# A state-space scan and a squared-ReLU FFN on one core: the first weight issue waits for the first x, the clamped later rows lie in PSUM, and the third unit's loads are let in later

## Chip, cores, metric

The kernel runs on one core of a Trainium2 chip. The metric is device time in microseconds of one execution; lower is better. Engines are called PE (TensorE), DVE (VectorE), ACT (ScalarE), POOL (GpSimd) and SP (SyncE, which here only issues DMAs).

## What is computed

Inputs are x (4 batches, 8 heads, 768 positions, 32 channels), a decay a, and B and C with 16 state elements each; then w_in (256 by 2048) and w_out (2048 by 256). Everything is float32.

```python
for c in range(nc):                              # chunks of 32 positions
    cum = np.cumsum(log(clip(a, 1e-6, 1)), -1)   # per chunk
    L = np.exp(cum_i - cum_j) * causal
    y = (C B^T * L) x + (C state) * exp(cum)
    state = exp(sum) * state + sum_j (B_j x_j) * exp(cum_end - cum_j)
h = np.maximum(y @ w_in, 0.0)                    # y as (3072, 256)
out = h * h @ w_out
```

## The kernel before

The sequence is cut into 12 **units**: 4 batches by 3 blocks of 256 positions, in the order of `UNITS` (first block of all four batches, then the second, then the third). Units 0 to 3 carry no incoming state. The decay enters as running products, not as exponents: `clamp` (L617) limits a to 1e-6..1, `scan` (L546) multiplies along 128 positions into `cp`, PE turns `cp` into columns (`prep_p`, L520 to L530), and the result `P_sb` and its reciprocal `Pinv` scale C and x. The rows of a come in two sets: 64 rows for the first block (`a_cl[0]`, `ac0`, `sk0`) and 128 rows for the later two blocks (`a_cl[1]`, `ac1`, `sk1`).

For one unit k the steps are: load C, B and x (`ldC`, `ldB`, `ldx`, tiles C_nat, B_nat, x_nat); multiply C by the decay and cast B into the tile `jt` (`pc`, L168, and `pb`, L176/L180); transpose `jt` on PE (`tr`, L206) and copy it to `bct` (`tc`, L219/L221); scores on PE (`mt`, L236); mask them, directly from PSUM on DVE (`mk`, L245) or from a copy `sc` (`sc`, L250, then `ms`, L254); scale x (`px`, L188, tile `xs`); the unit's own state (`u`, L261); the spread state `Sd` (`sf`, L389); intra matmuls in two halves (`ina`, `inb`) and the carried state (`ca`), all L261; copy the result to `T` (`t`, L219). Then the FFN of the unit's 256 positions in eight tiles: `a0` is tile 0 of unit 0's first matmul (L452, weights w_in_b) with its ReLU on ACT (L473), `qa0` the square on DVE (L479), `A0` the second matmul (L452, weights w_out_b). Unit 1 uses b and B, and so on. `id` are PE fillers on constants (L553).

Every engine runs its instructions in the order of the string `ORDER`; each token is one step, and a letter behind a colon names the engine. The order is therefore written by hand, and an engine that waits holds everything behind it. DMAs of C, B and x go out on SP's queue (a few on ACT's), those of the weights on POOL's, which converts to bf16 on the way: `wi0` to `wi3` are w_in_b0 to w_in_b3 (L149), `wo0` to `wo3` are w_out_b0 to w_out_b3 (L153).

Two devices delay a DMA on purpose. A **gate** (`gC2`, L144) clears one column of a unit's tile on DVE ahead of the load into that tile, so that the load cannot go out before DVE has come to that place. **After** (`afC2`, L669) copies one column of a loaded tile on POOL, so that what stands behind it on POOL waits for the load.

PSUM has eight banks in one tile `pp`; bank 4 holds the first block's decays (`P0`, columns 0 to 63) and sums (columns 64 to 71) until the token `fr`.

Of the kernel before, what the change touches and what calls it, by code (L numbers as in the profile page):

```python
# [10 lines left out]
FP32 = mybir.dt.float32  # L11
# [19 lines left out]
def kernel(  # L31
# [16 lines left out]
    ORDER = """  # L48
        fa1:a jz0:v ef jz1:p id3:512 ti fa0:s la0:s id4:512 pi eb ldB0:s ac0:v ldC0:a sk0 ku sp la1:a pbh0:p hd
        id1:256 pc0:v pbl0:v mb:a id2:512 trC0 ps iv:8:16 tcC0:1:a tcC0:0:v trB0 la2:s tcB0:2:v pk id1:512 iv1:0:8  # L50
        id1:512 ldx0:s mt0 wi0 la3:s px0:v ldC1:s su id2:512 ldB1:s wi1 ldx1:s u0:67 mk0 fq mk0 gC2:v mk0 ac1:v pc1:p sc0
        pb1:a jz2:a id2:512 tr1 id3:512 tc1:1:a tc1:0:v to ms0:p sf0 sk1 wo0 wi2 px1:p mt1 ina0 inb0 ca0 pp1:a mk1 mk1 t0:aa
        sc1 us0 mk1 fr p2@4 a0 ldC2:s a1 u1::6 ina1 ms1:v wo1 wi3 pc2 inb1 sf1 ca1 pd t1:va us1 a3@0 qa1 ldB2:s
        qa0 a2@1 wo2 b0@2 qa3 qb0 b1@3 qb1 b2@4 b3@5 A0 A1 B0 pb2:p B1 tr2 zb0 qb3 gB3:v ldx2:s ldB3:s ldC3:s ldx3:s b4 a4
        iv:32:64 zb1 tc2:1:v qa2 tc2:0:v b5 sb1 sb0 qb4 a5 qb2 qa4 mt2 sc2 B3 iv:16:32 px2 pc3 wo3 px3 mk2 mk2 sc2 A3
        A2 ms2:v ms2:v qa5 a6 b6 pb3:a B2 a7 qb5 qa6 b7 u2 ina2 inb2 sf2 ld4 A4 tr3 ca2 tc3:1:v t2:aa B4 us2 B5
        tc3:0:v u3:45 pc4 mt3 A5 us3 sc3 c5 qb7 qb6 mk3 za3 pb4 ldC5:s ldB5:s c3 qa7 c4 qc5 c0 qc3 px4 tr4 ldx5:s pb5
# [17 lines left out]
    const = ctx.enter_context(tc.tile_pool(name="const", bufs=1))  # L75
# [22 lines left out]
    spread = const.tile([128, 128], FP32, name="spread")  # L98

    a_nat = [const.tile([n, 128], FP32, name=f"a_nat{n}") for n in (64, 128)]  # L100
    a_cl = [const.tile([n, 128], FP32, name=f"a_cl{n}") for n in (64, 128)]
    cp = [const.tile([n, 128], FP32, name=f"cp{n}") for n in (64, 128)]
    pick_p = [const.tile([n, m], FP32, name=f"pick_p{n}") for n, m in ((64, 8), (128, 16))]
    P_sb = const.tile([128, 2, 96], FP32, name="P_sb")
# [5 lines left out]
    w_out_b = [wpool.tile([128, 4, 256], BF16, name=f"w_out_b{i}") for i in range(4)]  # L110

    pp = psum.tile([128, 8, 512], FP32, name="pp")

    def total(i, b, j):
        return 4 * i + b if j == 0 else 4 + 8 * i + 4 * j + b
# [757 lines left out]
```

## Time and profile before

| | |
|---|---|
| median of 3 runs | 114.65 us |
| lowest, highest run | 113.89, 118.19 us |
| span of the profiled execution, first to last instruction | 117.0 us |
| PE, DVE, ACT, POOL busy in it | 108.8, 85.9, 77.2, 49.6 us |
| mean granted PE clock | 0.985 |
| HBM read, written | 10.58, 3.15 MB |

No time of the profiled execution other than its span is on record, so the span stands for it; it lies 2.35 us above the median of the runs and within their reach.

A timeline row has the start, the duration, the engine, the line (L188 is line 188 of the listing), the operation, output <- inputs with shapes, the count of merged instructions, and in brackets the idle time of the engine just before it with what ended that. SPq and POOLq are the engines' DMA issues. In a row of a stretch (28.00:30.00) stand the length, then for PE, weight loads, DVE, ACT and POOL the busy time with the number of instructions, then the granted PE clock, the busy share of the DMA engines and GB/s. A row of a DMA issue ends in KB and the median microseconds from issue to landing. A row of the chain has start, length and what was worked on; the chain is followed back from the last instruction through what released each step.

### The profile page before, as it was taken

What the parts mean: (1) busy time and instruction counts of PE and PEld (TensorE: products, weight loads), DVE (VectorE), ACT (ScalarE), POOL (GpSimd) and SP (SyncE); (2) the same over time, 40 slices, a digit from 0 to 9 for tenths busy, and PEclk for the clock granted to TensorE, in tenths of its full rate; (3) what the DMA queues carried; (4) which work ended last, traced back from release to release, by engine and by line L of the source; (5) the groups of instructions that cost most, each with busy time, mean ns of one, the idle gap of its engine ahead of it and who ended that gap; (6) DMA issues with size and microseconds to landing.
All of it is one profiled execution on the core that took longest, in us unless ns stands there. A gap on an engine that the chain in (4) does not pass through costs nothing.

```text
span 117.0 us, 3689 instructions
## 1 busy us (share of the span) xinstructions
PE 108.8 (93%) x1453; PEld 92.9 (79%) x1453; DVE 85.9 (73%) x190; ACT 77.2 (66%) x159; POOL 49.6 (42%) x95
## 2 busy tenths in 40 slices
PE   7995998992999999999999999999999999999990
PEld 2542796882599898998998989989989889899980
DVE  2699965999469589799966799949849678544540
ACT  1582992972479478569566886786687777876740
POOL 7699434398088062396054294444333020000000
PEclk9999999999599999999999999999999999999999
DMA  2999999799997807697599737699790020020202
GB/s 44 200 208 147 201 205 223 139 217 161 94 169 101 236 6 107 72 215 85 75 171 98 137 104 93 71 191 97 124 198 34 0 98 0 0 95 0 88 2 90
DMA packets 67281, 13.44 MB, mean 115 GB/s; under 512 B 63104, under 2 KB 65984, under 8 KB 67264
## 3 DMA queue, kind: packets, MB, share of 16 engines
q1 hardware_dynamic: 64320, 10.88, 56.1%
q0 software_dynamic: 1664, 2.10, 11.0%
q10 hardware_dynamic: 1280, 0.23, 1.0%
q8 instruction: 11, 0.18, 0.6%
q14 instruction: 6, 0.05, 0.1%
HBM read 10.58 MB, written 3.15 MB: 117 GB/s over the span
## 4 chain that ended last, share of the span: by engine, by line
PE 77%; DVE 10%; DMA 9%; issue 1%; POOL 0%; SPq 0%; ACT 0%; DVEq 0%; ACTq 0%
PE pp L452 64%; DMA B_nat<-in_B_dram 9%; PE pp L261 5%; DVE h L479 5%; PE pp L553 4%; PE pp L230 2%; DVE mts L245 2%; PE pp L236 1%; DVE bct L221 1%; DVE mts L254 1%; DVE xs L188 1%; PE pp L206 1%; PE pp L530 0%; DVE Pinv L647 0%; POOL jt L176 0%
## 5 line engine op out<-in xcount | busy, mean ns | idle before, releaser
L473 ACT ACTIVATE hb<-pp 128x512 bf16<-128x512 f32 x96 | 54.7, 602 | 24.1 <-PE pp L452 22.2
L479 DVE TENSOR_TENSOR h<-hb 128x512 bf16<-128x512 bf16 x96 | 46.6, 502 | 13.3 <-ACT hb L473 12.8
L452 PE MATMUL pp<-w_out_b,h 128*128 128x256 bf16 (+1 forms) x400 | 54.8, 272 | 0.0
L452 PE MATMUL pp<-T,w_in_b 128*128 128x256 bf16 x384 | 53.4, 273 | 0.1
L452 PEld LDWEIGHTS <-w_in_b 128*128 128x128 bf16 x384 | 41.5, 114 | 1.9 <-issue 1.1
L452 PEld LDWEIGHTS <-h 128*128 128x128 bf16 x400 | 38.1, 99 | 5.0 <-issue 1.2
L245 DVE TENSOR_TENSOR mts<-pp,mask 128x512 bf16<-128x512 f32 x43 | 28.5, 678 | 2.7 <-PE pp L236 1.9
L188 POOL TENSOR_TENSOR xs<-x_nat,Pinv 128x256 bf16<-128x256 f32 (+1 forms) x19 | 13.6, 733 | 11.4 <-DVE mts L245 4.0
L377 POOL TENSOR_TENSOR Sd<-z,Pquad 128x256 bf16<-128x256 f32 x16 | 10.4, 657 | 18.0 <-DVE z L361 12.8
L168 POOL TENSOR_TENSOR jt<-C_nat,P_sb 128x128 bf16<-128x128 f32 x22 | 9.9, 469 | 6.9 <-DMA C_nat<-in_C_dram 6.8
L553 PE MATMUL pp<-const-bfloat16-1.0 128*128 128x512 bf16 (+1 forms) x19 | 6.9, 492 | 0.8 <-PEq L857 0.8
L176 POOL CAST jt<-B_nat 128x256 bf16<-128x256 f32 x9 | 4.2, 466 | 7.9 <-DMA B_nat<-in_B_dram 7.9
L361 DVE SCALAR_TENSOR_TENSOR z<-z,Ptot,us 128x64 f32<-128x64 f32 x8 | 2.5, 312 | 6.8 <-ACT us L345 5.0
L261 PE MATMUL pp<-bct,Sd 128*128 128x128 bf16 x40 | 4.3, 224 | 2.5 <-DVE Sd L389 2.5
L501 ACT COPY osb<-pp 128x512 f32<-128x512 f32 x11 | 6.4, 582 | 0.3 <-PE pp L452 0.2
L261 PEld LDWEIGHTS <-Sd 128*128 128x128 bf16 x40 | 3.0, 98 | 3.1 <-DVE Sd L389 2.9
L261 PE MATMUL pp<-mts,xs 64*32 64x128 bf16 (+1 forms) x288 | 5.5, 219 | 0.0
L261 PEld LDWEIGHTS <-xs 64*32 64x32 bf16 (+1 forms) x288 | 3.6, 93 | 0.4 <-issue 0.2
L553 PEld LDWEIGHTS <-const-bfloat16-1.0 128*128 128x128 bf16 x19 | 1.8, 116 | 2.5 <-issue 2.2
L250 ACT CAST sc<-pp 128x512 bf16<-128x512 f32 x5 | 2.9, 606 | 0.5 <-PE pp L236 0.5
L149 POOL DMA_DIRECT2D w_in_b<-in_moe_w_in_dram x4 | 3.0, 759 | 0.3 <-issue 0.3
L261 PEld LDWEIGHTS <-jt 64*32 64x32 bf16 (+1 forms) x128 | 1.5, 91 | 2.1 <-issue 1.2
(76 smaller groups left out, 61.0 us busy)
## 6 DMA issues: line engine op xcount, KB each, us to landing
out_dram<-osb SPq DMA_DIRECT2D x11, 256.0 KB, 2.9
x_nat<-in_x_dram SPq DMA_DIRECT2D x6, 256.0 KB, 4.3
w_in_b<-in_moe_w_in_dram POOLq DMA_DIRECT2D x4, 256.0 KB, 6.6
w_out_b<-in_moe_w_out_dram POOLq DMA_DIRECT2D x4, 256.0 KB, 6.6
B_nat<-in_B_dram SPq DMA_DIRECT2D x6, 128.0 KB, 3.5
C_nat<-in_C_dram SPq DMA_DIRECT2D x12, 64.0 KB, 3.0
B_nat<-in_B_dram SPq DMA_DIRECT2D x12, 64.0 KB, 3.4
x_nat<-in_x_dram SPq DMA_DIRECT2D x6, 128.0 KB, 3.0
```

The source lines that it names most:

```text
L149: nc.gpsimd.dma_start(out=w_in_b[i], in_=_dap(moe_w_in, f0 * 256, [[2048, 128], [128 * 2048, 2], [1, n]]))
L168: eng.tensor_tensor(out=_fap(jt[k % 3], 128 + 144 * g, [[384, 2], [32, 4], [1, 16]]), in0=_fap(loaded[k]["C"], 128 * g, [[16, 2], [32, 4], ...
L176: fn(out=_fap(jt[k % 3], 0, [[384, 2], [16, 2], [32, 4], [1, 16]]), in_=_fap(loaded[k]["B"], 0, [[16, 2], [128, 2], [32, 4], [1, 16]]))
L188: eng.tensor_tensor(out=_fap(xs, 256 * r, [[256, 2 // n], [32, 8], [1, 32]]), in0=_fap(loaded[k]["x"], 32 * r, [[32, 2 // n], [64, 8], [1, ...
L245: nc.vector.tensor_tensor(out=live[k]["mts"][:, q].rearrange("p r g i -> p (r g i)"), in0=pp[:, q, :], in1=mask1 if k >= LATE else mask, o ...
L261: nc.tensor.matmul(dst, w, v, start=bool(need), stop=False, skip_group_check=True, **({} if pos is None else {"tile_position": pos}))
L377: nc.gpsimd.tensor_tensor(out=_fap(S_d, 0, [[128, 2], [32, 4], [1, 32]]), in0=_fap(z, 0, [[32, 2], [0, 4], [1, 32]]), in1=_fap(Pquad, 4 * ...
L452: nc.tensor.matmul(dst, w(0, 128), v, skip_group_check=True, **flags)
L473: nc.scalar.activation(out=hb.rearrange("p i t -> p (i t)"), in_=pp[:, h, :], func=AF.Relu)
L479: nc.vector.tensor_tensor(out=h2, in0=hb, in1=hb, op=ALU.mult)
L501: nc.scalar.copy(out=osb, in_=pp[:, 6 if blk == 1 else 7, :])
L553: nc.tensor.matmul(pp[:, h, 0:int(cols)], ones_b[:, 0:128], ones_b[:, 0:int(cols)] if dep is None else dep, start=True, stop=True, skip_gr ...
```

## The change

Five edits, four of them in the string `ORDER`:

- `afx0` is put ahead of `wi0`: POOL copies a column of x_nat0 before it issues the first weights.
- `a_cl[1]`, the clamped 128 rows, is no longer an SBUF tile but columns 256 to 383 of PSUM bank 4.
- `px1` (xs of unit 1) is put ahead of `wi2`, and `u1` (unit 1's own state) ahead of `a1`.
- `wo2` follows `wi3` at once, ahead of `pc2`, where it stood behind it.
- `gC2`, `ldC2` move from early places (between unit 0's masks; ahead of `a1`) behind `sf1`, unit 1's spread state. In SP's queue B and x of unit 2 stand behind C_nat2.

```diff
-        id1:512 ldx0:s mt0 wi0 la3:s px0:v ldC1:s su id2:512 ldB1:s wi1 ldx1:s u0:67 mk0 fq mk0 gC2:v mk0 ac1:v pc1:p sc0
-        pb1:a jz2:a id2:512 tr1 id3:512 tc1:1:a tc1:0:v to ms0:p sf0 sk1 wo0 wi2 px1:p mt1 ina0 inb0 ca0 pp1:a mk1 mk1 t0:aa
-        sc1 us0 mk1 fr p2@4 a0 ldC2:s a1 u1::6 ina1 ms1:v wo1 wi3 pc2 inb1 sf1 ca1 pd t1:va us1 a3@0 qa1 ldB2:s
-        qa0 a2@1 wo2 b0@2 qa3 ...
+        id1:512 ldx0:s mt0 afx0 wi0 la3:s px0:v ldC1:s su id2:512 ldB1:s wi1 ldx1:s u0:67 mk0 fq mk0 mk0 ac1:v pc1:p sc0
+        pb1:a jz2:a id2:512 tr1 id3:512 tc1:1:a tc1:0:v to ms0:p sf0 sk1 wo0 px1:p wi2 mt1 ina0 inb0 ca0 pp1:a mk1 mk1 t0:aa
+        sc1 us0 mk1 fr p2@4 a0 u1::6 a1 ina1 ms1:v wo1 wi3 wo2 inb1 sf1 gC2:v ldC2:s pc2 ca1 pd t1:va us1 a3@0 qa1 ldB2:s
+        qa0 a2@1 b0@2 qa3 ...
...
-    a_cl = [const.tile([n, 128], FP32, name=f"a_cl{n}") for n in (64, 128)]
+    a_cl = [const.tile([64, 128], FP32, name="a_cl64")]
...
+    a_cl.append(pp[:, 4, 256:384])
```

What POOL runs, from the cast of unit 0's B to the cast of unit 2's B, before (the number behind a tile's name tells its copies apart; w_in_b_113 to _116 are w_in_b0 to w_in_b3, w_out_b_117 to _119 are w_out_b0 to w_out_b2):

```order
L180 CAST jt_110<-B_nat_144 128x2x4x16
L149 DMA w_in_b_113<-in_moe_w_in_dram 128x2x512
L149 DMA w_in_b_114<-in_moe_w_in_dram 128x2x512
L168 TENSOR_TENSOR jt_111<-C_nat_207,P_sb 128x2x4x16 x2
L254 TENSOR_TENSOR mts_202<-sc_3_242,mask 128x512
L153 DMA w_out_b_117<-in_moe_w_out_dram 128x1024
L149 DMA w_in_b_115<-in_moe_w_in_dram 128x2x512
L188 TENSOR_TENSOR xs_267<-x_nat_215,Pinv 128x512
L153 DMA w_out_b_118<-in_moe_w_out_dram 128x1024
L149 DMA w_in_b_116<-in_moe_w_in_dram 128x2x512
L168 TENSOR_TENSOR jt_112<-C_nat_236,P_sb 128x2x4x16 x2
L153 DMA w_out_b_119<-in_moe_w_out_dram 128x1024
```

The same stretch of POOL in the changed kernel (w_in_b_112 to _115 are w_in_b0 to w_in_b3, w_out_b_116 to _118 are w_out_b0 to w_out_b2):

```order
L670 COPY gate_x_202<-x_nat_183 128x1
L150 DMA w_in_b_112<-in_moe_w_in_dram 128x2x512
L150 DMA w_in_b_113<-in_moe_w_in_dram 128x2x512
L169 TENSOR_TENSOR jt_110<-C_nat_208,P_sb 128x2x4x16 x2
L255 TENSOR_TENSOR mts_201<-sc_3_241,mask 128x512
L154 DMA w_out_b_116<-in_moe_w_out_dram 128x1024
L189 TENSOR_TENSOR xs_265<-x_nat_216,Pinv 128x512
L150 DMA w_in_b_114<-in_moe_w_in_dram 128x2x512
L154 DMA w_out_b_117<-in_moe_w_out_dram 128x1024
L150 DMA w_in_b_115<-in_moe_w_in_dram 128x2x512
L154 DMA w_out_b_118<-in_moe_w_out_dram 128x1024
L169 TENSOR_TENSOR jt_111<-C_nat_404,P_sb 128x2x4x16 x2
```

One copy has come in ahead of the first weights; xs1 has moved ahead of w_in_b2; and w_out_b2 ahead of unit 2's C product, so that four weight issues now stand in a row. (Lines count one higher in the changed kernel from L113 on.)

What DVE runs from unit 0's second mask to unit 1's copy of T, before (C_nat_236 is C_nat2, Sd_0_405 unit 1's spread state):

```order
L245 TENSOR_TENSOR mts_202<-pp,mask 128x512
L144 MEMSET C_nat_236 128x1
L245 TENSOR_TENSOR mts_202<-pp,mask 128x512
L617 TENSOR_SCALAR a_cl_101<-a_nat_99 128x128
L221 COPY bct_248<-pp 128x384
L389 TENSOR_TENSOR Sd_0_262<-pp,Pquad 128x256
L546 SCALAR_TENSOR_TENSOR cp_103<-a_cl_101,const-float32-0.0 128x128
L245 TENSOR_TENSOR mts_285<-pp,mask 128x512 x3
L254 TENSOR_TENSOR mts_285<-sc_2_326,mask 128x512
L389 TENSOR_TENSOR Sd_0_405<-pp,Pquad 128x256
L221 CAST T_411<-pp 128x4x64
```

And in the changed kernel (C_nat_404 is C_nat2):

```order
L246 TENSOR_TENSOR mts_201<-pp,mask 128x512 x2
L618 TENSOR_SCALAR pp<-a_nat_99 128x128
L222 COPY bct_247<-pp 128x384
L390 TENSOR_TENSOR Sd_0_261<-pp,Pquad 128x256
L547 SCALAR_TENSOR_TENSOR cp_102<-pp,const-float32-0.0 128x128
L246 TENSOR_TENSOR mts_284<-pp,mask 128x512 x3
L255 TENSOR_TENSOR mts_284<-sc_2_325,mask 128x512
L390 TENSOR_TENSOR Sd_0_402<-pp,Pquad 128x256
L145 MEMSET C_nat_404 128x1
L222 CAST T_413<-pp 128x4x64
```

The memset on C_nat2 has moved behind eight instructions, and the scan reads `pp` and the constant where it read two SBUF tiles. On PE the sixteen matmuls of u1 and the four of a1 change places; ACT's and SP's orders stay as they were.

More of the change, by code (lines that the diff above doesn't have):

```diff
@@ L50 @@
         id1:256 pc0:v pbl0:v mb:a id2:512 trC0 ps iv:8:16 tcC0:1:a tcC0:0:v trB0 la2:s tcB0:2:v pk id1:512 iv1:0:8
-        id1:512 ldx0:s mt0 wi0 la3:s px0:v ldC1:s su id2:512 ldB1:s wi1 ldx1:s u0:67 mk0 fq mk0 gC2:v mk0 ac1:v pc1:p sc0
-        pb1:a jz2:a id2:512 tr1 id3:512 tc1:1:a tc1:0:v to ms0:p sf0 sk1 wo0 wi2 px1:p mt1 ina0 inb0 ca0 pp1:a mk1 mk1 t0:aa
-        sc1 us0 mk1 fr p2@4 a0 ldC2:s a1 u1::6 ina1 ms1:v wo1 wi3 pc2 inb1 sf1 ca1 pd t1:va us1 a3@0 qa1 ldB2:s
-        qa0 a2@1 wo2 b0@2 qa3 qb0 b1@3 qb1 b2@4 b3@5 A0 A1 B0 pb2:p B1 tr2 zb0 qb3 gB3:v ldx2:s ldB3:s ldC3:s ldx3:s b4 a4
+        id1:512 ldx0:s mt0 afx0 wi0 la3:s px0:v ldC1:s su id2:512 ldB1:s wi1 ldx1:s u0:67 mk0 fq mk0 mk0 ac1:v pc1:p sc0
+        pb1:a jz2:a id2:512 tr1 id3:512 tc1:1:a tc1:0:v to ms0:p sf0 sk1 wo0 px1:p wi2 mt1 ina0 inb0 ca0 pp1:a mk1 mk1 t0:aa
+        sc1 us0 mk1 fr p2@4 a0 u1::6 a1 ina1 ms1:v wo1 wi3 wo2 inb1 sf1 gC2:v ldC2:s pc2 ca1 pd t1:va us1 a3@0 qa1 ldB2:s
+        qa0 a2@1 b0@2 qa3 qb0 b1@3 qb1 b2@4 b3@5 A0 A1 B0 pb2:p B1 tr2 zb0 qb3 gB3:v ldx2:s ldB3:s ldC3:s ldx3:s b4 a4
         iv:32:64 zb1 tc2:1:v qa2 tc2:0:v b5 sb1 sb0 qb4 a5 qb2 qa4 mt2 sc2 B3 iv:16:32 px2 pc3 wo3 px3 mk2 mk2 sc2 A3
```

## The prediction

> **What bounds the kernel now.** I read the page's busy rows first, then the chain in order of time, then the stretches where TensorE (PE) is idle.
>
> ```profile
> span 117.0 us, 3689 instructions
> PE 108.8 (93%) x1453; PEld 92.9 (79%) x1453; DVE 85.9 (73%) x190; ACT 77.2 (66%) x159; POOL 49.6 (42%) x95
> PE   7995998992999999999999999999999999999990
> ```
>
> PE is idle for 117.0 - 108.8 = 8.2 us. The third row (busy tenths, slices of 2.9 us) shows where: before the first matmul, behind the last, and in three dips, the slices that begin at 8.8 (5), 17.5 (8) and 26.3 us (2). From the eleventh slice on PE is full. The change touches only the first 15 us, so the question is what it does to the dips. Pieces of the chain:
>
> ```profile
> 8.91 10.07 DMA B_nat<-in_B_dram
> ...
> 19.04 0.44 POOL jt L176
> ...
> 24.51 2.74 DVE h L479 x2
> ...
> 27.33 1.76 DVE h L479
> ...
> 29.48 0.39 PE pp L261 x2
> ```
>
> The reader is to see two things. From 8.91 to 18.98 the chain is the load of the third unit's B (B_nat2): it lands, POOL casts it into jt2 (L176), PE transposes jt2 (L206, "tr2"), and from there the chain is mostly work of VectorE (DVE) up to 29.48, where PE takes over for good. So **what moves the landing of B_nat2 moves the end**, and what PE gains ahead of 19 us is waited away again at tr2.
>
> ```profile
> 19.04 0.43 POOL L176 CAST jt<-B_nat 128x256 bf16<-128x256 f32 x1 [3.32 <-DMA B_nat<-in_B_dram]
> 19.52 0.51 PE L206 MATMUL pp<-eye_b,jt 128*128 128x128 bf16 x6 [0.57 <-POOL jt L176]
> 28.00:30.00 2.00, 0.52 (x4) 0.46 (x5) 2.00 (x5) 0.56 (x3) 0.81 (x2) 0.81 2.03 190
> 30.00:32.00 2.00, 2.00 (x40) 1.14 (x38) 0.62 (x2) 0.55 (x3) 0.00 (x0) 0.50 0.53 51
> ```
>
> PE waits only 0.57 us at tr2 now. Its largest wait is the hole before 29.48 (PE busy 0.52 of 2.00 us), after which the granted clock (the column behind POOL's) falls to 0.50.
>
> **The change, part by part.**
>
> *The gate on the first weights.* POOL now copies one column of x_nat0 before it issues w_in_b0.
>
> ```profile
> 2.81 0.43 SPq L135 DMA_DIRECT2D x_nat<-in_x_dram  x1
> x_nat<-in_x_dram SPq DMA_DIRECT2D x1, 256.0 KB, 3.1
> 5.34 1.63 POOL L149 DMA_DIRECT2D w_in_b<-in_moe_w_in_dram  x2 [0.26 <-issue]
> 36.28 0.38 POOL L669 COPY gate_C<-C_nat 128x1 f32<-128x1 f32 x1
> 6.99 0.80 POOL L168 TENSOR_TENSOR jt<-C_nat,P_sb 128x128 bf16<-128x128 f32 x2
> 7.75 1.15 POOL L254 TENSOR_TENSOR mts<-sc,mask 128x512 bf16<-128x512 bf16 x1
> 8.17 0.50 PE L206 MATMUL pp<-eye_b,jt 128*128 128x128 bf16 x6
> ```
>
> x_nat0 lands at 2.81 + 3.1 = 5.9; the copy takes 0.38 by the like one at L669; so the first issue goes from 5.34 to 6.3, **0.95 us later**. Queued behind it on POOL are the second issue, unit 1's C product (L168: ends 8.75 instead of 7.8), the mask of the copied scores (L254) and w_out_b0. PE waits for the C product: unit 1's transposes go from 8.17 to about 8.8. The mask ends near 9.85 instead of 8.9; the matmuls that use it stand behind those transposes and unit 1's scores on PE (over half a microsecond of work and a copy in between), which cover it; uncovered it would cost the same 0.95 us in a place ahead of tr2. The first weights landed 6.1 us after issue, at 11.4 (row further down); now at 12.4, or sooner by up to 0.9 if x_nat1 leaves the DMA engines earlier.
>
> *The clamped rows in PSUM.* The scan (L546) loses one operand in SBUF.
>
> ```profile
> 3.06 0.43 DVE L546 TENSOR_TENSOR_SCAN cp<-a_cl,const-float32-0.0 64x128 f32<-64x128 f32 x1
> 9.72 1.81 DVE L546 TENSOR_TENSOR_SCAN cp<-a_cl,const-float32-0.0 128x128 f32<-128x128 f32 x1
> 10.17 1.07 POOL L188 TENSOR_TENSOR xs<-x_nat,Pinv 128x512 bf16<-128x512 f32 x1
> 11.67 0.42 PE L520 MATMUL pp<-eye_f,cp 128*64 128x16 f32 x8 [1.12 <-DVE cp L546]
> 12.45 1.03 PE L452 MATMUL pp<-T,w_in_b 128*128 128x256 bf16 x8
> ```
>
> The same number of elements per row took 0.43 us while POOL computed nothing and 1.81 us across POOL's 1.07 us product. I take 0.45 for the scan from PSUM, near the first row, on the reading that POOL's reads held up the second one (bounds 0.43 and 1.81). So the scan starts 0.65 later (behind unit 1's transposes), at about 10.4, and ends at 10.85 instead of 11.5. PE's second set of decays (L520) follows it, and 0.8 us behind that the first FFN matmul, which could start at 11.8 instead of 12.45; but w_in_b0 lands between 11.5 and 12.4. **Gain ahead of the first FFN matmul: 0 to 0.6 us, I take 0.2**, and it ends at tr2's wait.
>
> *xs1, the state matmuls u1 and w_in_b2's issue.* These change places with what stood beside them.
>
> ```profile
> 15.11 0.61 POOL L153 DMA_DIRECT2D w_out_b<-in_moe_w_out_dram  x1
> ```
>
> An issue of w_out_b takes POOL 0.61 us, one of w_in_b 0.7 to 0.8. POOL's row now reads: C product, mask, w_out_b0 (to 10.4), xs1 (to 11.5), w_in_b2, w_out_b1, w_in_b3, w_out_b2 (to 14.2). xs1 is not earlier than now (11.24). w_out_b2, which stood behind the wait for C_nat2, goes out some 1.5 us sooner. Putting u1 (0.25 us of matmuls) ahead of the second FFN tile brings unit 1's state at most one tile (0.5 us) forward; it too is swallowed at tr2.
>
> *C_nat2's gate.* The one-column memset moves behind Sd1 on DVE.
>
> ```profile
> 8.49 0.37 SPq L135 DMA_DIRECT2D C_nat<-in_C_dram  x1
> 13.82 0.42 DVE L389 TENSOR_TENSOR Sd<-pp,Pquad 128x256 bf16<-128x256 f32 x1 [0.18 <-PE pp L261]
> C_nat<-in_C_dram SPq DMA_DIRECT2D x1, 128.0 KB, 5.5
> B_nat<-in_B_dram SPq DMA_DIRECT2D x1, 128.0 KB, 10.1
> w_in_b<-in_moe_w_in_dram POOLq DMA_DIRECT2D x1, 256.0 KB, 6.1
> ```
>
> SP's queue is in order: behind C_nat2 stand B_nat2 and x_nat2. All three leave **5.2 us later**: Sd1, a little sooner than now, ends at about 13.6, C_nat2 goes at 13.7, B_nat2 at 14.1 (0.42 behind it, as now: 8.49 and 8.91). Now C_nat2 lands at 14.0 and B_nat2 at 19.0. How late B_nat2 lands then depends on how SP's queue (q1) shares the DMA engines with the weights (q0). Packets, MB and share of 16 engines in four stretches: 8.5 to 10.5, 14.25 to 18, 10.5 to 12.25, and 20 to 21.5 us:
>
> ```profile
> q0 software_dynamic: 290, 0.28, 100.3%
> q1 hardware_dynamic: 4, 0.00, 0.4%
> ...
> q0 software_dynamic: 572, 0.68, 103.5%
> q1 hardware_dynamic: 459, 0.09, 20.4%
> ...
> q0 software_dynamic: 163, 0.18, 73.8%
> q1 hardware_dynamic: 892, 0.11, 42.4%
> ...
> q1 hardware_dynamic: 1739, 0.22, 94.7%
> ```
>
> A load of B or C is 128 KB at some 123 bytes a packet (892 packets for 0.11 MB), about 1050 packets. Alone, q1 moves 1739 in 1.5 us, so a load takes 0.9 us; beside dense weights it gets 0.8 packets for each of q0's (459 to 572); between two weight transfers it got 5.5 (892 to 163). C_nat2, issued at 8.49, had moved 4 packets at most by 10.5: the first packets come 2 us behind the issue.
>
> - *Floor*: q1 served at full rate. First packet at 15.7, two loads at 0.9 each: B_nat2 at 17.5, earlier than now.
> - *Ceiling*: 0.8 to one throughout. The weights flow from 8.3 (issue at 6.3 and 2 us) with q1 nearly empty, 0.14 MB each us (0.28 in 2 us): by 15.7 that is 1.04 MB, four transfers of the seven. Three, 0.79 MB, are left; at 0.68 MB in 3.75 us they take 4.4 us, to 20.1, in 660 packets. q1 moves 530 of its 2100 in that time, and the other 1570 in 1.4 us: 21.5.
> - *Taken*: 21.0, near the ceiling, since 14.25 to 18 is the stretch with several weight transfers queued, as POOL's four issues in a row will leave it.
>
> So B_nat2 lands at 21.0 instead of 19.0. C_nat2's product (0.8 us) runs while B_nat2 is moving. tr2 goes from 19.5 to **21.5, +2.0 us**; DVE's queue stands in order behind the copies of tr2, so everything to 29.48 shifts with it, and PE has no later idle time to take it back. What POOL's delay costs (0.65 us) and what the scan gains (1.36 us) both end ahead of tr2 and count for nothing; were B_nat2 no later, the cover would be gone and they would count.
>
> **Sum.** 117.0 + 2.0 = 119.0 us by the profiled execution's span, which lies 2.35 us above the median of the three runs (114.65). A shift of a wait carries over to them: 114.65 + 2.0 = **116.65 us**, by +1.7%.
>
> **Rivals.**
>
> 1. *B_nat2 lands no later than now.* For it: the 5.5 to one of 10.5 to 12.25, and that fewer weight packets are left when the loads start. Against it: 14.25 to 18. [...] Then PE's 0.57 us at tr2 falls away, and little more, since tr2 stands behind unit 0's and unit 1's FFN tiles: **114.0 us** (113.4 to 114.7).
> 2. *Slower: the longer wait costs the clock as well.* PE would idle from about 19.0 to 21.5. The hole before 29.48 (2.3 us, row below) was followed by a clock of 0.81 and 0.50 in the rows 28 to 30 and 30 to 32: 0.8 and 2.0 us at half rate, up to 1.4 us of work. It decides from a hole of about 2.3 us, thus if B_nat2 lands after 20.8: 116.65 + 1.4 = **118.05 us**. Against it: PE's backlog may then fill the later hole.
> 3. *Faster: the hole before 29.48 goes.* There DVE's squares take unusually long, next to a run of POOL's products:
>
> ```profile
> 24.43 4.66 DVE L479 TENSOR_TENSOR h<-hb 128x512 bf16<-128x512 bf16 x3
> 29.48 0.39 PE L261 MATMUL pp<-bct,Sd 128*128 128x128 bf16 x2 [2.30 <-DVE Sd L389]
> ```
>
>    Three squares take 4.66 us, where the mean of all 96 is 0.50 (46.6 us in the groups of the page). If the new timing pulls POOL's products and the squares apart, PE's 2.30 us is saved, without the shift: 114.65 - 2.3 = **112.3 us**. Against it: both engines hang on tr2 and shift together. [...]
> 4. *The scan is held by something else.* Then its 1.36 us stays, all of it ahead of tr2: the forecast's time, so no case of its own.
>
> **How the numbers follow.** The forecast has 0.43 (116.65, 115.6 to 117.7); rival 1 has 0.25, rival 2 0.16, rival 3 0.16. Two per cent of 114.65, about what a measurement of this kernel can tell from no change, is 2.3 us: 112.36 to 116.94. Faster: about two thirds of rival 3, and the part of it and of rival 1 in which both happen, 0.20. Slower: rival 2 and the upper part of the forecast (B_nat2 at its ceiling of 21.5 gives 117.15), 0.31. The rest, 0.49, is within. The range runs from rival 3's time to a microsecond over rival 2's, 112.3 to 119.0, since the low clock's 1.4 us may come with the ceiling.
>
> **What would show it.** In the profile after: w_in_b0's issue at 6.3 and its landing at 11.5 to 12.4; the scan at 0.45; C_nat2 issued near 13.7; POOL's cast of B_nat2 at 21.0 with a DMA wait ahead of it of several microseconds, and PE's L206 for unit 2 behind it with a wait of about 2.5. A cast at or before 19.0 would make the forecast wrong and rival 1 right; a clock below 1.00 between 20 and 27 would mean rival 2; squares near 0.5 between 24 and 31 rival 3.

## The result, and the profile after

The changed kernel takes **124.2 us** (median of 4 runs, 122.5 to 127.0) against 114.27 for the kernel before, and **a ratio of 1.076, interval 1.069 to 1.084**, slower. Executions come in a faster and a slower state, and every ratio here compares the faster ones alone (122.6 against 113.89 us, thus +8.7), while the execution of the changed kernel that was profiled (125.71) is one of the slower ones, some 3 us above the faster. Forecast were 116.65 us and at most 119.0.

The span of that execution ("after" below) is 124.0. A second profile of the unchanged kernel (called b0 below) has a span of 112.3 and a time of 114.02, near the median; the execution that the prediction read (span 117.0) was not a usual one, so after is set against b0 here. The parts of 11.7 us given below are those of this execution, not of the 8.7. First the heads of the two pages (busy tenths in 40 slices), after and then b0:

```profile
span 124.0 us, 3690 instructions
PE 110.3 (89%) x1453; PEld 93.1 (75%) x1453; DVE 85.0 (69%) x190; ACT 77.6 (63%) x159; POOL 48.7 (39%) x96
...
PE   7999980079948999999999999999999999999990
...
PEclk9999999657999999999999999999999999999999
```

```profile
span 112.3 us, 3688 instructions
...
PE   6998699999999999999999999999999999999990
```

In b0 PE is full from the sixth slice (14 us) on. After has a hole of two and a half slices from 18 us, a smaller one at 34 to 38 us, and a low granted clock in the slices from 22 to 31 us. The chain of after through these places (start, length, what was worked on):

```profile
13.15 11.11 DMA C_nat<-in_C_dram
...
24.42 0.76 POOL jt L169 x2
25.18 0.35 POOL jt L177
...
25.59 0.82 PE pp L207 x6
26.41 3.31 PE pp L453 x16
...
31.44 3.65 DVE mts L255 x2
35.10 2.33 DVE h L480 x3
...
37.82 0.28 PE pp L262 x2
```

It hangs on C_nat2, not on B_nat2: its load is under way for 11.1 us, then come the C product, the cast of B_nat2 and unit 2's transposes (tr2, L207). Rows of the timeline, after:

```profile
6.41 0.19 POOL L670 COPY gate_x<-x_nat 128x1 f32<-128x1 f32 x1 [1.01 <-DMA x_nat<-in_x_dram]
...
10.02 0.42 DVE L547 TENSOR_TENSOR_SCAN cp<-pp,const-float32-0.0 128x128 f32<-128x128 f32 x1
...
11.61 0.60 PE L453 MATMUL pp<-T,w_in_b 128*128 128x256 bf16 x4
...
13.15 0.37 SPq L136 DMA_DIRECT2D C_nat<-in_C_dram  x1
...
24.42 0.76 POOL L169 TENSOR_TENSOR jt<-C_nat,P_sb 128x128 bf16<-128x128 f32 x2 [10.21 <-DMA C_nat<-in_C_dram]
...
25.59 0.82 PE L207 MATMUL pp<-eye_b,jt 128*128 128x128 bf16 x6 [7.42 <-POOL jt L177]
...
31.36 3.74 DVE L255 TENSOR_TENSOR mts<-sc,mask 128x512 bf16<-128x512 bf16 x2
...
37.82 0.28 PE L262 MATMUL pp<-bct,Sd 128*128 128x128 bf16 x2 [1.39 <-DVE Sd L390]
```

The same places in b0:

```profile
8.24 0.37 SPq L135 DMA_DIRECT2D C_nat<-in_C_dram  x1
...
9.47 0.41 DVE L546 TENSOR_TENSOR_SCAN cp<-a_cl,const-float32-0.0 128x128 f32<-128x128 f32 x1
...
11.43 1.06 PE L452 MATMUL pp<-T,w_in_b 128*128 128x256 bf16 x8 [0.49 <-DMA w_in_b<-in_moe_w_in_dram]
...
17.87 0.60 POOL L176 CAST jt<-B_nat 128x256 bf16<-128x256 f32 x1 [2.03 <-DMA B_nat<-in_B_dram]
...
18.52 0.51 PE L206 MATMUL pp<-eye_b,jt 128*128 128x128 bf16 x6
```

In b0 tr2 comes without a wait; B_nat2 is just in time (the cast ends at 18.47). After waits 7.42 us there, and tr2 is 25.59 - 18.52 = 7.1 us later. Two stretches of after (PE busy, weight loads, DVE, ACT, POOL, clock, DMA share, GB/s):

```profile
26.00:28.00 2.00, 2.00 (x13) 1.50 (x12) 1.03 (x4) 0.60 (x1) 0.68 (x2) 0.50 1.03 198
28.00:30.00 2.00, 2.00 (x25) 1.12 (x23) 1.37 (x4) 1.44 (x3) 0.45 (x1) 0.63 1.26 171
```

At clocks of 0.50 and 0.63 these two stretches do 1.00 and 0.74 us less than full work; with the 0.41 us from tr2 to 26.00, also at a clock of 0.50, that is 1.95 us lost. **Where the 11.7 us went** (124.0 - 112.3): 7.1 at tr2, 1.95 to the low clock behind it, and 2.25 to waits at 34 to 38 us (1.39 in the row at 37.82; 0.54 and 0.32 just before, for the mask that DVE takes 3.74 us over beside POOL's products). That makes 11.3.

And the two queues (packets, MB, share of 16 engines): from 8.75 to 16.50 us, where SP's q1 has no row at all, and from 13.15 to 25.14, C_nat2's issue to the cast of B_nat2:

```profile
q0 software_dynamic: 891, 1.01, 95.1%
...
q0 software_dynamic: 905, 1.16, 60.2%
```

C_nat2, issued at 13.15, has not moved a packet by 16.50, and 1.16 MB of weights pass between its issue and the cast.

### The profile page after: what moved, and what is told of

It is laid out like the page before. It is cut to its first block, busy times and chain, and to the rows that moved or that the text cites. A ratio compares the mean times of both kernels' runs of the same rounds, so it can differ in the third digit from the quotient of the medians.

```text
span 124.0 us, 3690 instructions
## 1 busy us (share of the span) xinstructions
PE 110.3 (89%) x1453; PEld 93.1 (75%) x1453; DVE 85.0 (69%) x190; ACT 77.6 (63%) x159; POOL 48.7 (39%) x96
## 2 busy tenths in 40 slices
DMA packets 67281, 13.44 MB, mean 108 GB/s; under 512 B 63104, under 2 KB 65984, under 8 KB 67264
## 4 chain that ended last, share of the span: by engine, by line
PE 73%; DMA 12%; DVE 7%; POOL 3%; SPq 1%; ACT 1%; issue 1%; POOLq 0%; ACTq 0%
PE pp L453 62%; DMA C_nat<-in_C_dram 9%; PE pp L262 6%; DVE mts L255 3%; DMA x_nat<-in_x_dram 3%; DVE h L480 2%; PE pp L231 2%; PE pp L237 2%; POOL jt L169 1%; POOL w_in_b L150 1%; DVE mts L246 1%; PE pp L207 1%; SPq L656 1%; DVE Sd L390 1%; PE pp L554 1%
## 5 line engine op out<-in xcount | busy, mean ns | idle before, releaser
L453 PE MATMUL pp<-T,w_in_b 128*128 128x256 bf16 x384 | 55.2, 279 | 0.0
L453 PE MATMUL pp<-w_out_b,h 128*128 128x256 bf16 (+1 forms) x400 | 53.8, 268 | 0.0
L480 DVE TENSOR_TENSOR h<-hb 128x512 bf16<-128x512 bf16 x96 | 43.6, 467 | 14.3 <-ACT hb L474 13.6
L453 PEld LDWEIGHTS <-w_in_b 128*128 128x128 bf16 x384 | 42.0, 116 | 2.8 <-issue 1.1
L453 PEld LDWEIGHTS <-h 128*128 128x128 bf16 x400 | 37.6, 98 | 4.5 <-issue 1.0
L169 POOL TENSOR_TENSOR jt<-C_nat,P_sb 128x128 bf16<-128x128 f32 x22 | 9.1, 436 | 14.9 <-DMA C_nat<-in_C_dram 14.8
L207 PE MATMUL pp<-eye_b,jt 128*128 128x128 bf16 x24 | 2.5, 244 | 7.7 <-POOL jt L177 7.4
L207 PEld LDWEIGHTS <-jt 128*128 128x128 bf16 x24 | 1.9, 111 | 9.1 <-POOL jt L177 7.7
L222 DVE COPY bct<-pp 128x384 bf16<-128x384 bf16 (+1 forms) x7 | 2.2, 333 | 8.2 <-PE pp L207 8.2
L255 DVE TENSOR_TENSOR mts<-sc,mask 128x512 bf16<-128x512 bf16 x4 | 4.8, 1210 | 0.0
```

Of the source, the lines that this page charges most:

```text
L169: eng.tensor_tensor(out=_fap(jt[k % 3], 128 + 144 * g, [[384, 2], [32, 4], [1, 16]]), in0=_fap(loaded[k]["C"], 128 * g, [[16, 2], [32, 4], ...
L207: nc.tensor.transpose(pp[:, h, o:o + 64].bitcast(BF16), jt[k % 3][:, r, w, :], eye_b)
L255: eng.tensor_tensor(out=live[k]["mts"][:, q].rearrange("p r g i -> p (r g i)"), in0=live[k]["sc"][q], in1=mask, op=ALU.mult)
L453: nc.tensor.matmul(dst, w(0, 128), v, skip_group_check=True, **flags)
L480: nc.vector.tensor_tensor(out=h2, in0=hb, in1=hb, op=ALU.mult)
```

## The experiments

All are edits of `ORDER` (and the clamp's place). "Late gate" means C_nat2's gate and load behind `sf1`, as in the change.

**The gate undone.**

```diff
-... mk0 fq mk0 mk0 ac1:v ...   p2@4 a0 u1::6 a1 ...   sf1 gC2:v ldC2:s pc2 ca1
+... mk0 fq mk0 gC2:v mk0 ac1:v ...   p2@4 a0 ldC2:s u1::6 a1 ...   sf1 pc2 ca1
```

> The changed kernel with the memset and the load of C_nat2 alone back at their old places (memset between unit 0's masks, load ahead of u1); the other edits stay. Gate theory (the three loads of unit 2, issued 4.7 us later, wait behind weights that already fill the DMA engines): C_nat2 goes out near 8.5 and lands near 14, B_nat2 lands between 18 and 20, the wait of TensorE at unit 2's transposes is 2 us at most, time 113 to 115 us, ratio to before 0.99 to 1.01. Weights theory (w_out_b2 ahead of unit 2's C product and the later first issue make the weight queue dense, wherever the gate is): B_nat2 still lands after 22, the wait is over 4 us, time above 118 us.

114.7 us, ratio 1.008 (1.004 to 1.012). Its timeline:

```profile
8.60 0.37 SPq L136 DMA_DIRECT2D C_nat<-in_C_dram  x1
...
16.77 0.40 POOL L177 CAST jt<-B_nat 128x256 bf16<-128x256 f32 x1 [1.27 <-DMA B_nat<-in_B_dram]
...
18.54 0.50 PE L207 MATMUL pp<-eye_b,jt 128*128 128x128 bf16 x6
```

tr2 is back at 18.54 without a wait, and all but 0.8% of the loss is gone. **The late gate is the cause** of all but that.

**The gate alone**, in the kernel before (`pc2` and `wo2` keep their order behind it):

```diff
-mk0 gC2:v mk0 ...   a0 ldC2:s a1 ...   wo1 wi3 pc2 inb1 sf1 ca1
+mk0 mk0 ...   a0 a1 ...   wo1 wi3 inb1 sf1 gC2:v ldC2:s pc2 ca1
```

> The kernel before with one edit: the memset and the load of C_nat2, and with them unit 2's C product (and w_out_b2 behind it), stand behind unit 1's spread state. Gate theory: C_nat2 goes out near 13.9, lands after 20, TensorE waits over 4 us at unit 2's transposes, time 119 to 123 us, ratio 1.04 to 1.08. Weights theory: w_out_b2 still stands behind C_nat2's landing, so the loads meet two weight transfers fewer and land by 18; time below 116 us, ratio below 1.02.

119.71 us, ratio 1.050 (1.044 to 1.056).

```profile
18.86 0.76 POOL L168 TENSOR_TENSOR jt<-C_nat,P_sb 128x128 bf16<-128x128 f32 x2 [5.95 <-DMA C_nat<-in_C_dram]
20.64 0.51 PE L206 MATMUL pp<-eye_b,jt 128*128 128x128 bf16 x6 [2.40 <-POOL jt L176]
...
25.55 4.78 DVE L479 TENSOR_TENSOR h<-hb 128x512 bf16<-128x512 bf16 x3
...
30.72 0.40 PE L261 MATMUL pp<-bct,Sd 128*128 128x128 bf16 x2 [2.42 <-DVE Sd L389]
```

The time is as the gate theory had it, the wait is not: C_nat2's product starts at 18.86 and not after 20, and PE waits 2.40 us and not over 4. Here tr2 is only 2.1 us late, close to the 2.0 that the prediction gave, and yet the span is 118.2, 5.9 above b0's. The rest comes behind tr2: DVE's squares take 4.78 us for three, PE waits 2.42 us before 30.72, and the mean clock of 0.986 over 118.2 us means up to 1.65 us lost. The sum, 2.1 + 2.4 + 1.65 = 6.2, is near the 5.9. Of the 1.65 less than one us seems to count in the time: three executions with a clock of 0.986 took 119.60 to 119.95 us, the fourth, with 1.000, took 119.02. So **a late tr2 costs several us more behind it**, and the gate alone costs less than the whole change.

**The clamp alone**, in the kernel before:

```diff
-    a_cl = [const.tile([n, 128], FP32, name=f"a_cl{n}") for n in (64, 128)]
+    a_cl = [const.tile([64, 128], FP32, name="a_cl64")]
+    a_cl.append(pp[:, 4, 256:384])
```

> The kernel before with one edit: the clamped 128 rows in PSUM. Both theories: the scan takes 0.42 us instead of 1.81, the first FFN matmul stands 1.0 to 1.4 us earlier than 12.45. If B_nat2's landing sets the end, as in the prediction, this gain is waited away at unit 2's transposes: 113.3 to 114.5 us, ratio 0.99 to 1.00. If TensorE's own row ahead of 19 us counts instead, the whole 1.0 to 1.4 us comes through: 112 to 113 us, ratio 0.985 to 0.99.

114.79 us, ratio 1.000 (0.995 to 1.005): nothing. The scan takes 0.41 us, as it does from SBUF in b0. The first FFN matmul, expected 1.0 to 1.4 us ahead of 12.45, stands at 12.40 in its profile, behind a wait of 1.26 us for w_in_b.

**The first weights' wait alone** (`mt0 wi0` to `mt0 afx0 wi0` in the kernel before):

> The kernel before with one edit: the copy of x_nat0 ahead of the first weight issue. This looks for the 0.8 per cent by which the changed kernel with its gate put back is still slower than before. If the later weights cost it: first weights issued near 6.5, first FFN matmul or a later weight waited for, ratio 1.005 to 1.01, 114.5 to 115.2 us. If they do not: ratio 0.997 to 1.004.

115.4 us, ratio 1.012 (1.008 to 1.017).

```profile
10.99 0.42 PE L236 MATMUL pp<-bct 32*64 32x256 bf16 x16 [0.90 <-DVE bct L221]
...
19.26 0.50 PE L206 MATMUL pp<-eye_b,jt 128*128 128x128 bf16 x6
```

Unit 1's scores wait, and tr2 comes at 19.26, 0.74 later than in b0. The cost is about what stayed over in the first experiment; but there, with the same wait for x, tr2 was not late (18.54), so where its 0.8% is lost is not shown.

**Both undone** (the first experiment, and `afx0` taken out):

> The changed kernel with C_nat2's gate and load where they were and without the first weights' wait for x: the clamp in PSUM, px1 ahead of wi2, u1 ahead of a1 and wo2 ahead of inb1 stay. Theory (the two gates are the whole cost): the time is the kernel before's, ratio 0.99 to 1.004, about 114.0 us; first weights issued at about 5.4, first FFN matmul at 11.5 to 12.4, tr2 at about 18.5 with no wait. Rival (another step costs the 0.8% that stayed when the C_nat2 gate alone was undone): ratio 1.006 to 1.012, 115 us, with tr2 or first FFN matmul later than the kernel before has it.

114.56 us, ratio 1.005 (1.001 to 1.010). This lies between the theory's upper end (1.004) and the rival's lower one (1.006), and the interval holds both, so it is not settled whether the first weights' wait explains the whole 0.8%. In its profile the first FFN matmul waits 0.81 us for w_in_b and comes at 12.02, tr2 at 19.49; whether that belongs to this order or to this execution stays open.

**C_nat2 with no gate at all**, behind x1's load, and no wait for the first weights:

> As e10_both_gates_back, but C_nat2's load stands right behind x1's with no gate at all, issued at about 6 instead of 8.2 to 8.6. Theory (the end hangs on tr2, and tr2 no longer waits for B_nat2 once it lands by about 17): nothing to gain at tr2, which stays at 18.2 to 18.6; ratio 0.99 to 1.003. Rival (C_nat2 and B_nat2 now share the DMA engines with the first weights, which the first FFN matmul waits for): the first FFN matmul at 12.0 to 12.6 instead of 11.5, tr2 at 19 or later, ratio 1.005 to 1.01.

114.02 us, ratio 1.0005 (0.997 to 1.004): as the theory had it, though the first FFN matmul comes at 12.19, as the rival had it. Issued at 5.80 instead of 8.24, C_nat2 gains nothing, since tr2 (18.59) does not wait for it. No kernel here beats the one before.

### Why the same gate costs 5% alone and 7.6% in the change

**w_out_b2 late again**, in the changed kernel (`wo2` behind `pc2`):

> The changed kernel with w_out_b2 alone back behind unit 2's C product, so that one weight transfer fewer is queued when C_nat2 goes out. Gate theory: the loads still come after w_out_b1 and w_in_b3; C_nat2 lands 1 to 3 us sooner than in the changed kernel (24.3), time 119 to 122 us, ratio 1.04 to 1.07. Weights theory (the dense row of four issues is the cause): C_nat2 lands by 17, time below 116 us.

123.35 us, ratio 1.082 (1.074 to 1.089); tr2 at 24.15. C_nat2 lands at 22.2, 2 us sooner as the gate theory had it, but the time does not fall to its 119 to 122. w_out_b2's place alone is not the difference.

**Weights held back**, in the changed kernel:

```diff
-ms1:v wo1 wi3 wo2 inb1 ...   B0 pb2:p B1 tr2
+ms1:v inb1 ...   B0 pb2:p wo1 wi3 wo2 B1 tr2
```

> The changed kernel, with the late gate, but the issues of w_out_b1, w_in_b3 and w_out_b2 held on POOL until unit 2's B is cast, so that C_nat2 and B_nat2 meet at most the tail of w_in_b2. Queue theory (the loads are late because they share the DMA engines, packet by packet, with weights that were queued ahead): C_nat2, issued near 13.2, lands by 17.5 and B_nat2 by 18.5, TensorE waits under 1.5 us at unit 2's transposes, time 113.5 to 116.5 us (the held weights may add a wait of their own later). Lateness theory (what is issued at 13.2 lands some 8 to 11 us later whatever else is queued): C_nat2 after 21, time above 118 us.

118.17 us, ratio 1.037 (1.025 to 1.048). The third row is of the queues from C_nat2's issue to the cast of B_nat2 (13.44 to 19.17):

```profile
18.41 0.80 POOL L169 TENSOR_TENSOR jt<-C_nat,P_sb 128x128 bf16<-128x128 f32 x2 [5.74 <-DMA C_nat<-in_C_dram]
19.61 0.51 PE L207 MATMUL pp<-eye_b,jt 128*128 128x128 bf16 x6 [0.63 <-POOL jt L177]
...
q0 software_dynamic: 356, 0.39, 44.0%
...
23.68 1.47 PE L453 MATMUL pp<-w_out_b,h 128*128 128x256 bf16 x12 [1.45 <-DMA w_out_b<-in_moe_w_out_dram]
```

With 0.39 MB of weights in the way instead of 1.16, C_nat2 lands 4.8 us behind its issue instead of 11.1, and tr2 comes 6.0 us sooner, although the gate is as late. The price is then paid at 23.68 and again at 26.47 by PE, which waits for the weights held back, so the time misses the theory's 113.5 to 116.5 us. What delays C_nat2 is weights in the same DMA engines; C_nat2 was expected at 17.5 or sooner, so even 0.39 MB costs more than the theory had.

**Which part of the change brings the weights there?** Five kernels with the late gate. The changed kernel without `afx0`:

> The changed kernel without the first weights' wait for x; the late gate of C_nat2 stays. Theory (the weights, started 1.0 us later, stand more densely in the way of C_nat2, and this makes the difference between 1.050 for the late gate alone and 1.076 for the whole change): C_nat2 issued at 12.5 to 13.5, landed at 18.5 to 20.5, tr2 at 20.5 to 22, ratio 1.045 to 1.058. Rival (the interaction is with px1, u1 or wo2, which stay): C_nat2 lands at 22 or later, tr2 at 24 or later, ratio 1.068 or more.

123.68 us, ratio 1.087 (1.077 to 1.097), tr2 at 23.97: **the theory on the first weights' wait falls.** Its C_nat2 came in time (product at 20.23), but the cast then waited 2.53 us for B_nat2. Next, `wi2` ahead of `px1` again, first with and then without `afx0`:

> The changed kernel with wi2 issued ahead of px1 again; all else of the change stays. Theory (px1 holds the weight issues back into the way of C_nat2): wi2 issued at about 10.6 instead of 11.6, wo1 and wi3 about as before, so part of the interaction goes: C_nat2 lands at 19 to 22.5 instead of 24.3, tr2 at 21 to 24, ratio 1.05 to 1.07. Rival (the swap has no part in it): C_nat2 at 22 or later, ratio 1.074 or more.

> The changed kernel without the first weights' wait for x and with wi2 issued ahead of px1 again; the late gate, the clamp, u1 and wo2 stay. Theory (px1 ahead of wi2 is the interaction): wi2 issued at 9.9 as in e2_gate_only, C_nat2 landed at 18.5 to 20, tr2 at 20.5 to 21.5, ratio 1.044 to 1.06. Rival (u1's earlier place or the clamp): C_nat2 at 20 or later, tr2 at 23 or later, ratio 1.075 or more, as with e11_no_x0_gate.

124.2 us, 1.090 (1.085 to 1.096), and 123.31 us, 1.086 (1.079 to 1.094): the swap is not needed for it either. The swap alone beside the late gate, in the kernel before:

> The kernel before with C_nat2's late gate, as e2_gate_only, and px1 ahead of wi2; nothing else of the change. Theory: wi2 is issued behind px1, which waits for x1, at about 12.5 instead of 9.9, wo1 and wi3 at 13 to 14.5; C_nat2 lands at 20 to 22 instead of 18.8, tr2 at 22.5 to 24, ratio 1.07 to 1.09. Rival (the swap has no part in it): as e2_gate_only, tr2 at 20.5 to 21, ratio 1.044 to 1.056.

122.49 us, ratio 1.066 (1.059 to 1.072): not needed, but enough for a part. Then u1's place with the clamp, and w_out_b2's place, each without the rest of the change beside the late gate (measured together, where the kernel before took 115.35 us at the least, against 113.06 to 113.45 in the other sets of runs; so their ratios are low, and the two are best compared with each other):

> The kernel before with C_nat2's late gate (as e2_gate_only), the clamp in PSUM and u1 ahead of a1; the weights are issued as in the kernel before, wo2 late. Theory (only weights issued close to C_nat2 make it worse): if C_nat2 is issued 1 us or more behind wi3, tr2 at 20 to 21 and a ratio of 1.04 to 1.06 as in e2_gate_only; if the earlier u1 and the shorter scan bring its issue to within 0.5 us of wi3's, tr2 at 22 or later and 1.065 or more. Rival (the clamp or u1 costs by itself, wherever the weights stand): tr2 at 22 or later with the issues apart.

> The kernel before with C_nat2's late gate (as e2_gate_only) and wo2 issued ahead of inb1; nothing else of the change. Theory: wo2 is issued at about 12.9, 0.7 us ahead of C_nat2, and C_nat2 lands at 20.5 to 22.5 instead of 18.8, tr2 at 22 to 24, ratio 1.065 to 1.09. Rival (wo2 has no part in it, as e4_wo2_back suggested): tr2 at 20.5 to 21, ratio 1.044 to 1.056.

119.77 us, ratio 1.031 (1.017 to 1.045), and 123.42 us, ratio 1.065 (1.054 to 1.075). u1 and the clamp add nothing (119.71 us for the gate alone, in another set); w_out_b2 ahead of C_nat2's product has 3.65 us more than they have, so it is enough by itself, although taking it out of the change (above) did not help. The rule by distance, that a weight issued within 0.5 us of C_nat2 makes the bad case, falls with the first of these: its weight stands 0.49 us ahead, and its tr2 is at 21.22. What goes with the delay is how many MB of weights pass between C_nat2's issue and the cast of B_nat2. Three of the rows (the gate alone, then these two), and the table, whose fifth column is the time of the one execution that the columns before it were read from:

```profile
q0 software_dynamic: 551, 0.65, 62.0%
...
q0 software_dynamic: 763, 0.91, 66.7%
...
q0 software_dynamic: 647, 0.86, 61.0%
```

| late gate, and | weights, MB | C_nat2's issue to the cast, us | tr2, us | that execution, us | ratio |
|---|---|---|---|---|---|
| whole change, weights held | 0.39 | 5.7 | 19.61 | 118.14 | 1.037 |
| nothing else | 0.65 | 6.6 | 20.64 | 119.95 | 1.050 |
| swap of px1 and wi2 | 0.83 | 8.9 | 23.41 | 123.51 | 1.066 |
| wo2 early | 0.86 | 9.0 | 23.10 | 122.93 | 1.065 |
| whole change, wo2 late | 0.90 | 10.3 | 24.15 | 125.78 | 1.082 |
| u1, clamp | 0.91 | 8.2 | 21.22 | 119.83 | 1.031 |
| whole change, no afx0 | 1.05 | 9.7 | 23.97 | 122.69 | 1.087 |
| the same, no swap either | 1.10 | 9.5 | 22.44 | 122.57 | 1.086 |
| whole change, no swap | 1.15 | 10.2 | 24.03 | 124.17 | 1.090 |
| whole change | 1.16 | 12.0 | 25.59 | 125.71 | 1.076 |

A straight line through the ten has 2.9 us and 6.8 us per MB (each point within 1.4 us), about the 7.1 us per MB at which q0 moves alone (0.28 MB in 2 us, in the prediction's row). C_nat2 and B_nat2 fare nearly **as if they stood behind all the weights that are on their way**. The MB are not large merely because the stretch is long: the weights issued by C_nat2's issue or within 1.1 us behind it (0.262 MB each), less what had moved by its issue, come to the same figures within 0.05 MB. The line is for loads issued behind the weights. With the gate early, where B_nat2's cast also waits for its load (the first profile of the kernel before, b0, the gate undone), 1.51, 1.29 and 1.09 MB pass, and the stretches of 10.55, 9.63 and 8.17 us are 2.0 to 2.6 us shorter than the line. The swap and w_out_b2 put more weights on the way; they stand in for each other, so undoing one leaves the wait, and with both undone and no `afx0` (the row of u1 and the clamp) tr2 is back at 21.22, near the gate alone's 20.64. The rule is read from ten profiles, one each, and the ratio does not follow the MB (1.031 at 0.91); why the line is not closer stays open.

The table has one thing more. The time of the execution less tr2 is 98.5 to 101.6 us in these ten, and 95.4 to 96.9 in the profiles with the gate early (b0 95.5), save the first one of the kernel before (about 99). So with the late gate 3 to 6 us more come behind tr2, whether it is 1.1 or 7.1 us late; in the kernel with the weights held these are mostly waits for weights.

**Is it the clock?** 28 fillers of 512 columns ahead of tr2 in the changed kernel (`B1 tr2` to `B1 id28:512 tr2`):

> The changed kernel with 28 filler matmuls of 512 columns (6.0 us at full clock) put ahead of unit 2's transposes, into TensorE's wait of 7.4 us; no result uses them. If half clock behind the wait costs time: the granted clock stays at 1.00 from 20 to 30 us and the time falls by 1 to 2.5 us, to 120 to 121.5 us (ratio 1.05 to 1.065). If the low clock lies where VectorE is the slower one anyway: the time stays at 122 to 124 us, ratio 1.07 to 1.08.

125.12 us, ratio 1.081 (1.068 to 1.095): no gain. Of its four executions two had a mean granted clock of 1.000 and took 123.36 and 123.89 us, two had 0.973 and took 126.36 and 126.62; the profile is of one of the latter:

```profile
25.01 0.51 PE L207 MATMUL pp<-eye_b,jt 128*128 128x128 bf16 x6 [0.64 <-POOL jt L177]
...
24.00:30.00 6.00, 5.37 (x63) 4.44 (x62) 4.45 (x12) 3.53 (x7) 4.04 (x8) 1.00 1.13 179
...
35.00:42.00 7.00, 6.01 (x58) 3.86 (x59) 3.83 (x10) 3.34 (x8) 3.35 (x8) 0.51 0.90 135
```

There the clock stays at 1.00 across tr2, and falls to 0.51 behind the later hole instead, where PE waits 3.32 us for Sd. In the other two it did not fall at all, and they are still no shorter than the changed kernel's 122.5 and 122.7 us, at clocks of 0.984 and 0.970. So the low clock is not what makes the change cost 8.7 us. What it costs by itself is not settled by this kernel: where the wait is shorter than in the profile, the 6.3 us of fillers may hold tr2 back.

**The kernel before once more:**

> The kernel before, unchanged, for a profile of an execution near its median: the first profile had a span of 117.0 us, above the runs' median of 114. Expected: span near 112, no stretch of low clock, unit 2's transposes at or before 18.5 us with no wait of over 0.6 us. If instead its transposes stand near 19.5 as in the first profile, the hole ahead of 29.5 us must be shorter.

114.02 us; its rows are shown with the result.

## Why the prediction was wrong

- **The bound: right in place, wrong in slack.** The chain does go through unit 2's loads and tr2, and PE's gain ahead of it was waited away, as said. But the 0.57 us of wait at tr2, the hole of 2.30 us before 29.48 and the low clock belong to the one execution read; b0 has none of the three. A span is 1.7 us below the time of its execution (112.3 and 114.02, 124.0 and 125.71), so the one read took about 118.7 us, longer than any of the three runs (113.89 to 118.19). The shift was added to a base in which hole and clock were already paid; in a usual run the change brings them in, and its tr2 stands at 18.52, so that even a cast at 21.0 would have made tr2 3.0 us late and not 2.0. **What follows a late tr2 was put at nothing**, on the ground that everything behind it only shifts: in after it is 1.95 + 2.25 = 4.2 us of the 11.7, and with the gate alone, where tr2 is as late as forecast, 3.8 of the 5.9.
- **The landing of B_nat2: the step that failed.** The ceiling was 21.5 and 21.0 was taken, so tr2 was to be 2.0 us late; the cast ran at 25.14, and tr2 was 7.1 us late. The weights still to move were sized well (0.79 MB forecast at the first packet, 0.77 measured from 16.50 on). Three terms were too small and a fourth was left out, as these rows show (the two queues from 16.50 to 21.70, then the busy tenths of the DMA engines from 21.70 to 25.30 in slices of 0.09 us, and q1 in the same stretch):

```profile
q0 software_dynamic: 546, 0.73, 82.5%
q1 hardware_dynamic: 1320, 0.18, 27.2%
...
DMA  9999999999989787764423122100000000369999
...
q1 hardware_dynamic: 2378, 0.42, 62.2%
```

  The first packet came at 16.5, at least 3.35 us behind the issue and not 2.0: 0.8 us over the ceiling's 15.7. The weights took 5.2 us from there, not 4.4: another 0.8. From 21.7 on C_nat2 still needed 2.6 us, where 1.4 was to be enough for both loads: 1.15. The DMA engines are full to 22.7 and nearly idle from 23.6, yet C_nat2 lands at 24.26; from 23.6 to 24.3 q1 moves 110 packets in 15.2% of the engines' time, and why so few at a time no row shows. Then the C product stands ahead of the cast: 0.9. With the 0.5 from 21.0 to the ceiling that is 4.15, the whole way to 25.14. These figures are of one execution; in the other nine of the table the cast came 5.7 to 10.3 us behind the issue, where the forecast's 13.7 and 21.0 allow 7.3. The packet ratio on which the ceiling rested (0.8 to one) was not the mistake: q1 got 2.4 packets for each of q0's (1320 to 546). The stretch taken for q1 alone (20 to 21.5 us) also had 28 packets of q0, which changes little.
- **C_nat2 and not B_nat2 is last.** The C product was costed as hidden; with C_nat2 landing at 24.26 it stands in the chain (0.76 us, and the cast behind it). In three of the other kernels (no afx0, the swap alone, wo2 early alone) the chain goes through B_nat2 instead, as forecast.
- **POOL's row and the first weights: right.** Copy at 6.41, first issue at 6.53 (forecast 6.3), C_nat2 at 13.15 (13.7). The 6.3 is close by luck in part: x_nat0 lands at 6.35 and not 5.9, and the copy takes 0.19 us and not 0.38. The delay of the first weights was costed at nothing, hidden by tr2's wait. That holds in the change; without the late gate it is 1.2%.
- **The scan: right number, wrong comparison.** It takes 0.42, forecast 0.45, but b0 has 0.41 from SBUF: the 1.81 was the exception. The row of 0.43 was misread too: POOL did compute during it, selects of 0.20 us at 3.02 and 3.29 and one of 0.29 at 3.45. In b0 POOL computes nothing during the scan; in the gate alone's profile the scan takes 0.67 and runs for 0.22 into POOL's product of x. Here the stretch came only beside that product, but not each time: with the first weights' wait alone the product (from 11.35) runs beside 0.24 us of the scan (from 11.18), and the scan takes 0.41. No profile has a scan from PSUM beside it, so the reading that POOL held the scan up, and that PSUM spares it, was the author's and is not shown.
- **Rivals.** 1 (no later) is excluded by the row at 24.42. 2 (the clock falls too) happened: 0.50 and 0.63 in the rows 26 to 30, 1.95 us instead of 1.4 (which left out the stretch from 32 to 34 us of the first profile, at a clock of 0.84). It was given a chance of its own, 0.16, though the hole it needs comes with the forecast itself. 3 went the other way: in b0 there was no hole to be removed, and with the late tr2 it comes. In after POOL works from 29.55 to 36.8 us nearly without a break beside DVE's masks and squares, and two masks there take 3.74 us, where one took 0.41 at 12.26; whether POOL's work makes the hole is not shown. The cost (PE waits of 1.4 to 3.3 us before a unit's carried state) was seen in all the profiles with a late gate save the one with the weights held. The late gate is not its only cause: with the gate early the wait was 2.30 us in the first profile of the kernel before, 1.32 in the clamp alone's and 0.76 in that of the first weights' wait alone, each with tr2 at 19.26 to 19.66.

## To carry to other kernels

Before moving a load later, count the MB of other queues' transfers that will be in the DMA engines at its new place, and let it wait for all that are issued ahead of it or just behind it (here 2.9 us and 6.8 us per MB, from ten profiles); the share that it got in another stretch was no guide here (0.8 packets to one of q0, then 2.4). Price a wait that newly opens on the bounding engine with what follows it, which here was another 3 to 6 us (in after 1.95 of low clock and 2.25 of waits). Look whether the execution read is a usual one (its span against the median) before taking its holes as given.

## What the runs showed of the hardware

- C_nat2 in after, issued at 13.15 while weights took 81.5% of the DMA engines' time (0.40 MB up to 16.50), showed no packet for 3.35 us. Its product began 5.0, 5.3 and 11.3 us behind the issue, with 0.39, 0.65 and 1.16 MB of weights passing up to the cast of B_nat2.
- All 44 executions with a late gate have a mean clock of 0.999 to 1.000, 0.984 to 0.986, 0.969 to 0.973 or 0.958 to 0.959. At the 0.50 of after's row from 26 to 28 us, the means of 0.986 over 118.2 us and 0.972 over 124.0 us are 3.3 and 6.9 us of low clock. What sets these lengths is not shown, nor is a length of hole from which the clock falls: with the gate alone it stayed at 1.00 from 20 to 26 us, behind the wait of 2.40 us at tr2, and fell to 0.60 and 0.55 in the stretches 30 to 32 and 32 to 34 us, behind the wait of 2.42.
- With 6.3 us of fillers in PE's wait the clock was 1.00 from 24 to 30 us, and two executions with them had 1.000 throughout; the time was not shorter (123.36 and 123.89 us).
